# Seven products of halves for z1 in a Fourier-mixing and gated-MLP layer, with h2 stored turned

## The chip, the cores and the metric

The kernel runs on one core of one Trainium2 chip. The time is the device time of one execution in microseconds (us), as the median of several runs. The engines are TensorE (PE in the profile; its weight loads PEld), VectorE (DVE), ScalarE (ACT), GpSimd (POOL) and SyncE (SP), which only issues transfers.

## The reference

Sequence 2048, width 512, fp32. The two parts and what lies around them, cut:

```python
mod = (silu(c) @ w_mod).reshape(1, 6, 1, -1)          # sa, ca, ga, sb, cb, gb
h = layernorm(x) * (1 + ca) + sa
y = dft_seq_re @ (h @ dft_hid_re.T) - dft_seq_im @ (h @ dft_hid_im.T)
x = x + ga * y
h = layernorm(x) * (1 + cb) + sb                       # "h2" in the kernel
z = gelu(h @ w_in)                                     # 512 -> 1792
z1, z2 = z[..., :896], layernorm(z[..., 896:])
g = w_sp @ z2 + b_sp[:, None]                          # w_sp is 2048 x 2048
x = x + gb * ((z1 * g) @ w_out)                        # 896 -> 512
```

## The kernel before

Each fp32 product is made of three matmuls on a high and a low part (`matmul3`: high x high, high x low, low x high). The high part is an ACT copy to the PE's rounded type (`ah` of a streamed block, `prep_hi`), the low part a DVE subtraction (`al`, `prep_lo`); both stand in small rings of buffers. The names carry the block's number: al131 is the low part of block 131.

The streamed blocks are numbered n, and TensorE works through them in order. Blocks 0 to 127 (N2 = 128) are the DFT stage: `mm_a(n)` multiplies h by a block of the sequence DFT matrices, four quarters t of 512 tokens. For each tile (t, i) of 128 tokens, `mm_y` multiplies by the width DFT; then `post_y` adds x and takes statistics (DVE, with the factors on POOL), `norm_y` applies them (ACT), and `post_h` multiplies and adds the modulation (DVE, then POOL) and stores the tile of h2. The tiles of the quarters t = 0 to 2 are done between later blocks; those of t = 3 come after block 127, at N2 - 0.25, one after the other.

Then z1 (N2 to N3): h2's quarters are loaded back and turned by DVE as 128 x 512 blocks (`turn_block`), since the contraction must lie on partitions; 4 quarters x 7 column chunks x 4 k x 3 matmuls. Then z2 (N3 to N4), in seven products of halves (`mm_z2`), and w_sp times z2, also in seven products (`mm_w`); the sums of w_sp's quarters that this needs are made ahead in 16 units (`load_s`, `sum_s`), stored to `s_d` and streamed back. Last comes the product with w_out (`mm_o`).

The order is written out by hand: `at(n, f, ...)` puts a step behind block n, and `run(n)` emits what is due. Each engine runs its instructions in this order, so a step that waits holds back what is behind it on its engine. The buffers of the stages follow each other in the same memory: `change_s` closes the row buffers of the DFT stage and opens the slots of the later stages.

Of the passage into z1 these lines set the place of al131 (N2 + 3), for i = 2 and 3 of the last quarter:

```python
if i == 2:
    at(N2 - 0.25, prep, N2)
if i == 3:
    at(N2 - 0.25, prep_lo, N2 + 3)
at(N2 - 0.25, post_y, t, i)
at(N2 - 0.25, norm_y, t, i)
at(N2 - 0.25, post_h, t, i)
```

Of the kernel before, what the change touches and what calls it, by code (L numbers as in the profile page):

```python
# [19 lines left out]
def fnet_gmlp_kernel(  # L20
# [62 lines left out]
    h2_d = [dram.tile([Q, D], F32, name=f"h2_d{t}") for t in range(NQ)]  # L83
# [56 lines left out]
    src += h2_d + h2_d[:1]  # L140
    N3 = N2 + 4 * NQ
# [5 lines left out]
    NB = {p: N4 + 4 * NQ * i for i, p in enumerate(PROD)}  # L147
    stage, T, AH, AL = {}, {}, {}, {}
# [37 lines left out]
    def turn_block(dst, b, k):  # L186

        nc.vector.transpose(dst.rearrange("p (k a i) -> p a k i", k=4, i=32),
                            stage[b][:, :, 32 * k:32 * k + 32].rearrange("p (a k) i -> p a k i", k=4))
        if k == 3:  # L190
            stage.pop(b)
            load(b + 2)

# [3 lines left out]
    slots, TT, S2 = [], {}, {}  # L197

    def again(k):
        TT[k, 0] = slot(12 + k, f"tt0_{k}")  # L200
        turn_block(TT[k, 0], len(src) - 1, k)

    def form3(gg, kk):
        t = TT[kk, gg]
        nc.vector.tensor_tensor(t, TT[kk, 2 + gg], t, op=ALU.subtract)

    def prep_hi(n):
        if n >= NE:
            return
        if N3 <= n < N4:  # L210
            p = ZPROD[(n - N3) // 4]
            gg, kk = divmod((n - N3) % 4, 2)
            if p == 6:
                T[n] = S2[gg, kk] = bpool[0].tile([P, Q], F32, tag=("bh", "bl")[kk], bufs=3, name=f"s2_{gg}{kk}")
                nc.vector.tensor_tensor(T[n], TT[2 + kk, gg], TT[kk, gg], op=ALU.subtract)
            else:
                T[n] = TT[kk + (2 if p in (2, 4, 3) else 0), gg + (2 if p in (1, 2, 5) else 0)]
        else:
            b, k = divmod(n, 4) if n < N3 else (len(src) + (n - N4) // 4, (n - N4) % 4)
            if N2 + 4 <= n < N3:  # L220
                g = (n - N2) // 4
                T[n] = TT[k, g] = slot(4 * g + k - 4, f"tt{g}_{k}")
            else:
                T[n] = blocks.tile([P, Q], F32, tag="t", bufs=2, name=f"t{n}")
            if n >= N4:
                squares(T[n], stage[b][:, k % 2], k // 2)
            elif n < N2:
                squares(T[n], stage[b], k)
            else:
                turn_block(T[n], b, k)  # L230
        AH[n] = blocks.tile([P, Q], F32R, tag="ah", bufs=4, name=f"ah{n}")
        nc.scalar.activation(AH[n], T[n], AF.Copy)  # L232
        if not N2 <= n < N4 and k == 3:
            stage.pop(b)
            load(b + 2)
# [3 lines left out]
    def prep_lo(n):  # L239
# [3 lines left out]
        if N3 <= n < N4 and (n - N3) % 4 == 3:  # L243
            AL[n] = slot(16, f"al{n}", F32R)
# [295 lines left out]
    def post_h(t, i):  # L540
# [3 lines left out]
        nc.gpsimd.dma_start(h2_d[t][i * P:(i + 1) * P, :], h2)  # L544


    wi_hi, wi_lo, wraw, ZT = {}, {}, {}, {}
    z_hi, z_lo, Z, ZN = {}, {}, {}, {}

    WJ, W2 = {}, []  # L550

    def load_wi(e, k0):

        if e == 0:
            raw = wpool[0].tile([P, 2, FH], F32, tag="wj", bufs=2, name=f"wraw{k0}")
        else:
            if not W2:
                W2.append(wpool[0].tile([P, ND, FH], F32, name="w2"))
            raw = W2[0][:, k0:k0 + 2, :]
        v = w_in.rearrange("(a k i) f -> a i k f", a=4, i=32)  # L560
        for a in range(4):
            nc.sync.dma_start(raw[32 * a:32 * a + 32], v[a][:, k0:k0 + 2, e * FH:(e + 1) * FH])
        if e == 0:
            for k in range(2):
                wraw[k0 + k] = raw[:, k, :]

    def make_wi(k):
        wi_hi[k] = wpool[1].tile([P, FH], F32R, name=f"wih{k}")
        wi_lo[k] = wpool[1].tile([P, FH], F32R, name=f"wil{k}")
        nc.scalar.activation(wi_hi[k], wraw[k], AF.Copy)  # L570

    def make_wi_lo(k):
        nc.vector.tensor_tensor(wi_lo[k], wraw.pop(k), wi_hi[k].bitcast(F32), op=ALU.subtract)
# [3 lines left out]
    def parts_w2():  # L577
        w = W2[0]
        return w[:, :2, E0], w[:, :2, E1], w[:, 2:, E0], w[:, 2:, E1]

    def form_w23():
        b11, b12, b21, b22 = parts_w2()
        nc.vector.tensor_tensor(b12, b22, b12, op=ALU.subtract)
        nc.vector.tensor_tensor(b11, b11, b12, op=ALU.add)

    def form_w14():
        t2, _, b21, b22 = parts_w2()
        W2.append(wpool[0].tile([P, 2, ZP], F32, name="w2s"))
        nc.vector.tensor_tensor(W2[1], b22, t2, op=ALU.subtract)
        nc.vector.tensor_tensor(t2, b21, t2, op=ALU.subtract)  # L590

    def form_w(p):
        return W2[1] if p == 5 else parts_w2()[{1: 0, 6: 0, 7: 1, 2: 2, 4: 0, 3: 3}[p]]

    def hi_w(p):
        WJ[p] = wpool[0].tile([P, 2, 2, Q], F32R, tag="wj", bufs=2, name=f"wj{p}")
        nc.scalar.activation(WJ[p][:, 0, :, :ZP], form_w(p), AF.Copy)

    def lo_w(p):
        hi, lo = WJ[p][:, 0, :, :ZP], WJ[p][:, 1, :, :ZP]  # L600
        nc.vector.tensor_tensor(lo, form_w(p), hi.bitcast(F32), op=ALU.subtract)

    def mm_z1(ns):
        g, k0 = divmod(ns[0] - N2, ND)
        if k0 == 0:
            for f in range(NF):
                ZT[f] = bank((NF * g + f) % 8, f"z1p{g}_{f}")
        a = [(k0 + m, AH.pop(n), AL.pop(n)) for m, n in enumerate(ns)]
        for f in range(NF):
            cols = slice(f * P, (f + 1) * P)  # L610
            for k, th, tl in a:
                matmul3(ZT[f], wi_hi[k][:, cols], wi_lo[k][:, cols], th, tl, k == 0, k == ND - 1)
        if k == ND - 1:
            for f in range(NF):
                z = zrow[0].tile([P, Q], F32, tag="z1row", bufs=NF, name=f"z1_{g}_{f}")
                nc.scalar.activation(z.rearrange("p (a k i) -> p k a i", a=4, i=32),
                                     ZT.pop(f).rearrange("p (k a i) -> p k a i", k=4, i=32), AF.Gelu_apprx_tanh)
# [52 lines left out]
    def sum_s(r, g, b, first):  # L670
        a11, a12, a21, a22 = [SJ[r, g, b][:, i] for i in range(4)]
# [39 lines left out]
    def mm_w(n):  # L711
# [206 lines left out]
    for j, load_at, n, m, k, plus_one in ((2, 41, 49, 50, 7, False), (4, 52, 56, 58, 7, True),  # L918
                                          (3, 60, 65, 66, 7, False), (5, 68, 85, 86, 6, False)):
# [5 lines left out]
    for t in range(NQ):  # L925
        n = 8 * NQ * (t + 1)
        for i in range(4):
# [7 lines left out]
            if t < NQ - 1:  # L935
                at(y + 1, post_y, t, i)
                at(y + 2, norm_y, t, i)
                at(y + 3 if t else 71 + i, post_h, t, i)
                if i < 2:
                    at(y + 2 if t else y + 3, load_xr, t, i + 2)  # L940
            else:
                if i == 2:
                    at(N2 - 0.25, prep, N2)
                if i == 3:
                    at(N2 - 0.25, prep_lo, N2 + 3)
                at(N2 - 0.25, post_y, t, i)
# [30 lines left out]
    at(90, change_q)  # L977
    at(N2, change_s)
    when = [(90 + 4 * i, 3) for i in range(9)] + [(N2 + d, 6) for d in (4, 7, 10, 13, 17, 21, 25)]
# [10 lines left out]

    at(N2 + 1, load_wi, 1, 0)
    at(N2 + 2, load_wi, 1, 2)
    at(N2 + 6, hi_w, 1)
    at(N2 + 7, lo_w, 1)
    at(N2 + 9, form_w23)
    at(N2 + 10, hi_w, 6)
    at(N2 + 10, lo_w, 6)
    at(N2 + 12, form_w14)
    for k, d in ((0, 10), (2, 11), (1, 12), (3, 13)):
        at(N2 + d, again, k)  # L1000
    for gg in range(2):
        for kk in range(2):
            at(N2 + 14 + gg, form3, gg, kk)
            at(N3 + 4 + 2 * gg + kk, form1, gg, kk)
    for n in range(N2, N3):
        prep(n)
        run(n)
        two_first(mm_z1, n, n - N2, ND)
# [76 lines left out]
    for o in range(len(order)):  # L1085
# [53 lines left out]
```

## Time and profile before

| | us |
|---|---|
| median of 3 runs | 949.32 (948.85 to 950.26) |
| the profiled execution | 948.71 |
| its span | 946.8 |
| PE busy in the span | 938.3 (99%) |
| DVE / ACT / POOL busy | 712.3 / 391.7 / 168.2 |
| z1, from its first to its last matmul | 448.2 to 524.4 |
| z2 | 524.4 to 593.7 |

The span is the part of the execution that the profile's instructions cover; 1.9 us lie around it. The granted clock of TensorE is 1.0 throughout. In the rows of the profile a line such as L248 is the line of the kernel, "al<-t,ah" is what is written and read, x244 the number of instructions; in a time line the bracket gives the idle time before an instruction and what ended it.

### The profile page before, as it was taken

The page shows a single profiled execution, that of the slowest core. Times are in us where ns is not written, and L with a number is a line of the kernel's source. Part 1 is how long each engine was busy: PE and PEld are TensorE (multiplying, and loading weights), DVE is VectorE, ACT ScalarE, POOL GpSimd, SP SyncE. Part 2 cuts the span into 40 slices and gives each one's busy share as a digit, 9 for nine tenths or more (in the row PEclk, how much of TensorE's full clock was granted, in tenths as well). Part 3 has the DMA queues.
Part 4 walks back from the last instruction along what each step waited for, and adds up shares of the span by engine and source line. Part 5 has one row for each costly group of instructions (what it writes and reads, how often), then busy time and mean ns, then how long its engine had stood idle before and what let it go on. Part 6 is the DMA issues. An engine that isn't in the chain of part 4 may idle for free.

```text
span 946.8 us, 12325 instructions
## 1 busy us (share of the span) xinstructions
PE 938.3 (99%) x4150; PEld 778.9 (82%) x4150; DVE 712.3 (75%) x1156; ACT 391.7 (41%) x680; POOL 168.2 (18%) x330
## 2 busy tenths in 40 slices
PE   8999999999999999999999999999999999999998
PEld 5888888888888888888888998888888888888886
DVE  6789957775566767876537778999799889886662
ACT  4685424242132222322433768765545444331221
POOL 2330000111520154223412421332000000000000
PEclk9999999999999999999999999999999999999999
DMA  9996662667435877993887920544555465744541
GB/s 203 223 224 127 136 145 67 167 164 180 134 100 144 246 225 212 283 324 144 230 315 225 373 117 20 133 91 102 143 125 121 101 155 118 195 103 153 180 176 55
DMA packets 243343, 158.11 MB, mean 167 GB/s; under 512 B 130000, under 2 KB 212176, under 8 KB 243152
## 3 DMA queue, kind: packets, MB, share of 16 engines
q1 hardware_dynamic: 231520, 119.70, 51.7%
q0 software_dynamic: 11424, 37.24, 10.6%
q8 instruction: 32, 0.52, 0.2%
q10 hardware_dynamic: 336, 0.39, 0.1%
q14 instruction: 31, 0.25, 0.1%
HBM read 120.59 MB, written 36.70 MB: 166 GB/s over the span
## 4 chain that ended last, share of the span: by engine, by line
PE 97%; DVE 1%; ACT 1%; DMA 1%; POOL 0%; issue 0%; SPq 0%; DVEq 0%
PE gp L96 12%; PE gp L97 12%; PE gp L95 12%; PE gw L97 10%; PE gw L96 10%; PE gw L95 10%; PE yp L95 3%; PE yp L97 3%; PE yp L96 3%; PE op L96 3%; PE op L95 3%; PE z1p L97 3%; PE z1p L95 3%; PE op L97 3%; PE z1p L96 3%; PE z2p L97 2%
## 5 line engine op out<-in xcount | busy, mean ns | idle before, releaser
L232 ACT ACTIVATE ah<-t 128x512 fp32r<-128x512 f32 x244 | 154.0, 632 | 373.6 <-DVE t L175 234.7
L248 DVE TENSOR_TENSOR al<-t,ah 128x512 fp32r<-128x512 f32 x244 | 164.8, 676 | 70.9 <-PE gp L96 45.5
L95 PE MATMUL gp<-ah,hh 128*128 128x512 f32 x496 | 192.9, 389 | 0.0
L96 PE MATMUL gp<-al,hh 128*128 128x512 f32 x496 | 192.9, 389 | 0.0
L97 PE MATMUL gp<-ah,hl 128*128 128x512 f32 x496 | 192.9, 389 | 0.0
L175 DVE STREAM_TRANSPOSE t<-stage 128x512 f32<-128x512 f32 x240 | 168.9, 704 | 9.5 <-DMA stage<-in_A_dft_seq_re_dram 4.1
L97 PE MATMUL gw<-ah,bl 128*128 128x512 f32 x400 | 155.8, 390 | 0.3 <-DVE bl L709 0.3
L96 PE MATMUL gw<-al,bh 128*128 128x512 f32 x400 | 155.7, 389 | 0.0
L95 PE MATMUL gw<-ah,bh 128*128 128x512 f32 x400 | 155.6, 389 | 0.0
L95 PEld LDWEIGHTS gp<-ah,hh 128*128 128x128 f32 x496 | 93.1, 188 | 19.4
L97 PEld LDWEIGHTS gp<-ah,hl 128*128 128x128 f32 x496 | 93.1, 188 | 19.3
L96 PEld LDWEIGHTS gp<-al,hh 128*128 128x128 f32 x496 | 93.1, 188 | 19.3
L97 PEld LDWEIGHTS gw<-ah,bl 128*128 128x128 f32 x400 | 75.1, 188 | 16.4 <-DVE bl L709 1.0
L96 PEld LDWEIGHTS gw<-al,bh 128*128 128x128 f32 x400 | 75.1, 188 | 15.7
L95 PEld LDWEIGHTS gw<-ah,bh 128*128 128x128 f32 x400 | 75.1, 188 | 15.6
L681 POOL DMA_DIRECT2D s_d<-sj x64 | 34.8, 544 | 130.1 <-DVE sj L673 97.2
L248 DVE TENSOR_TENSOR al<-tt,ah 128x512 fp32r<-128x512 f32 x36 | 23.9, 683 | 38.6 <-PE z1p L96 28.6
L95 PE MATMUL yp<-hth,gh 128*128 128x512 f32 x128 | 49.8, 389 | 0.0
L96 PE MATMUL yp<-htl,gh 128*128 128x512 f32 x128 | 49.8, 389 | 0.0
L97 PE MATMUL yp<-hth,gl 128*128 128x512 f32 x128 | 49.8, 389 | 0.0
L95 PE MATMUL z1p<-ah,wih 128*128 128x512 f32 x112 | 43.6, 389 | 0.0
L96 PE MATMUL z1p<-al,wih 128*128 128x512 f32 x112 | 43.6, 389 | 0.0
(171 smaller groups left out, 1400.8 us busy)
## 6 DMA issues: line engine op xcount, KB each, us to landing
stage<-in_A_dft_seq_im_dram SPq DMA_DIRECT2D x64, 256.0 KB, 5.3
sj<-in_B_w_sp_dram SPq DMA_DIRECT2D x32, 512.0 KB, 7.3
s_d<-sj POOLq DMA_DIRECT2D x64, 256.0 KB, 4.9
stage<-s_d SPq DMA_DIRECT2D x128, 128.0 KB, 2.7
stage<-in_A_dft_seq_re_dram SPq DMA_DIRECT2D x60, 256.0 KB, 5.0
stage<-in_B_w_sp_dram SPq DMA_DIRECT2D x96, 128.0 KB, 3.3
z_d<-z POOLq DMA_DIRECT2D x28, 256.0 KB, 5.7
stage<-h_d SPq DMA_DIRECT2D x20, 256.0 KB, 6.7
```

Source lines behind the costliest of these rows:

```text
L95: nc.tensor.matmul(acc, ah, bh, start=first, stop=False, skip_group_check=go_on)
L96: nc.tensor.matmul(acc, ah, bl, start=False, stop=False, skip_group_check=go_on)
L97: nc.tensor.matmul(acc, al, bh, start=False, stop=last, skip_group_check=go_on)
L175: nc.vector.transpose(dst.rearrange("p (b i) -> p b i", i=32), block[:, :, 32 * k:32 * k + 32])
L232: nc.scalar.activation(AH[n], T[n], AF.Copy)
L248: nc.vector.tensor_tensor(AL[n], t, AH[n].bitcast(F32), op=ALU.subtract)
L681: nc.gpsimd.dma_start(s_d[m, r, g][b * P:(b + 1) * P, :], a)
```

## The change

- The first six of z1's seven column chunks are made by seven products of halves (`YPROD`), with three chunks, two halves of the tokens (gg) and two k blocks each. The sums of h2's quarters that they need (`form_t`, `make_x`) are those that z2 uses too, and stay in the slots; the sums of the weights are made by `form_v`. The seventh chunk stays a plain product (`mm_f7`), fitted between them. z1 now has 28 blocks and 300 matmuls, where it had 16 blocks and 336.
- PSUM results of the products 1, 6 and 7 are copied out by ACT; product 2 is followed by six copies back into PSUM, which product 4 goes on from; products 5 and 3 are added by DVE.
- h2 is stored turned: `turn_h` transposes a finished tile on DVE into `hturn` (one buffer) and stores it by four POOL transfers of 64 KB, in pieces of 128 bytes, to `ht_d` [width, tokens]. Before, `post_h` stored it by one POOL transfer. z1's blocks are then loaded as they are, and the twenty DVE transposes of `turn_block` go.
- The low parts of blocks N2 + 3, N2 + 7 and so on to N4 use slot 0, which exists only after `change_s`; `change_s` is called once the DFT stage is written out.
- w_in's halves are loaded as natural rows, two transfers for each half.
- Eleven of the 16 w_sp units are in the DFT stage (from n = 82, every 4 blocks; nine from n = 90 before), and the last modulation row is summed at 74 and 76.
- The columns of w_sp's quarters, the order of PSUM banks and two loads of w_sp are changed to fit.

On DVE, at the passage from the DFT stage into z1 (h2_3_i is tile i of the last quarter, y its y, xr its x, mod4 the modulation, wil the low part of a weight), before:

```order
L542 TENSOR_TENSOR h2_3_2_4145<-h2_3_2_4145,mod4_2060 128x512
L573 TENSOR_TENSOR wil2_4151<-wraw2_4068,wih2_4150 128x896
L573 TENSOR_TENSOR wil3_4155<-wraw2_4068,wih3_4154 128x896
L248 TENSOR_TENSOR al131_4158<-t131_4121,ah131_4128 128x512
L531 TENSOR_TENSOR y3_3_4160<-yp3_3_0_4027,mod2_1784 128x512
L532 TENSOR_TENSOR xr3_3_4115<-y3_3_4160,xr3_3_4115 128x512
L103 BN_STATS bsty_4164<-xr3_3_4115 128x6
L105 BN_AGGR mvy_4166<-bsty_4164 128x2
L542 TENSOR_TENSOR h2_3_3_4173<-h2_3_3_4173,mod4_2060 128x512
```

and after (vj is a part of a product's weights, w7 the seventh chunk's):

```order
L557 TENSOR_TENSOR h2_3_2_4205<-h2_3_2_4205,mod4_2060 128x512
L606 TENSOR_TENSOR vj2_4215<-w1_4135,vj2_4215 128x2x384
L614 TENSOR_TENSOR w7_4185<-w1_4135,w7_4185 128x256
L546 TENSOR_TENSOR y3_3_4220<-yp3_3_0_4099,mod2_1784 128x512
L547 TENSOR_TENSOR xr3_3_4183<-y3_3_4220,xr3_3_4183 128x512
L103 BN_STATS bsty_4224<-xr3_3_4183 128x6
L105 BN_AGGR mvy_4226<-bsty_4224 128x2
L564 STREAM_TRANSPOSE hturn3_2_4235<-h2_3_2_4205 128x512
L557 TENSOR_TENSOR h2_3_3_4233<-h2_3_3_4233,mod4_2060 128x512
L564 STREAM_TRANSPOSE hturn3_3_4243<-h2_3_3_4233 128x512
L265 TENSOR_TENSOR al131_4261<-xb0_3845,ah131_4188 128x512
```

al131 stood ahead of the last tile's five instructions; now it stands behind them and behind the turns of the last two tiles.

On POOL, the same place (nmry is the last factor of a tile's statistics), before:

```order
L115 TENSOR_SCALAR nmry_4143<-mvy_4138,rsy_4140 128x1
L543 TENSOR_TENSOR h2_3_2_4145<-h2_3_2_4145,mod3_2270 128x512
L544 DMA h2_d3_83<-h2_3_2_4145 128x512
L533 DMA x2_d3_79<-xr3_3_4115 128x512
L107 TENSOR_SCALAR mvy_4166<-mvy_4166 128x1
L108 TENSOR_TENSOR rsy_4168<-mvy_4166,mhalf_122 128x1
L115 TENSOR_SCALAR nmry_4171<-mvy_4166,rsy_4168 128x1
L543 TENSOR_TENSOR h2_3_3_4173<-h2_3_3_4173,mod3_2270 128x512
L544 DMA h2_d3_83<-h2_3_3_4173 128x512
```

and after:

```order
L567 DMA ht_d3_83<-hturn3_1_4207 32x16x32 x4
L558 TENSOR_TENSOR h2_3_2_4205<-h2_3_2_4205,mod3_2270 128x512
L548 DMA x2_d3_79<-xr3_3_4183 128x512
L107 TENSOR_SCALAR mvy_4226<-mvy_4226 128x1
L108 TENSOR_TENSOR rsy_4228<-mvy_4226,mhalf_122 128x1
L115 TENSOR_SCALAR nmry_4231<-mvy_4226,rsy_4228 128x1
L567 DMA ht_d3_83<-hturn3_2_4235 32x16x32 x4
L558 TENSOR_TENSOR h2_3_3_4233<-h2_3_3_4233,mod3_2270 128x512
L567 DMA ht_d3_83<-hturn3_3_4243 32x16x32 x4
```

Each tile's store is four transfers for one, and the store of a tile stands ahead of the next tile's addition.

On TensorE, after, where the second half of the first product begins (f7p0 is the seventh chunk of the first quarter):

```order
L97 MATMUL f7p0_4292<-ah129_3972,w7_4185 128x512
L95 MATMUL z1p1_10_4319<-ah130_3992,vj1_4157 128x512
L96 MATMUL z1p1_10_4319<-al130_4190,vj1_4157 128x512
L97 MATMUL z1p1_10_4319<-ah130_3992,vj1_4157 128x512
L95 MATMUL z1p1_10_4319<-ah131_4188,vj1_4157 128x512
L96 MATMUL z1p1_10_4319<-al131_4261,vj1_4157 128x512
```

Ahead of the first row stand z1's first 23 matmuls, on the blocks 128 and 129; al131 is read by the 29th. Before, the blocks 128 and 129 had all seven chunks, 42 matmuls.

The diff, cut:

```diff
-        nc.gpsimd.dma_start(h2_d[t][i * P:(i + 1) * P, :], h2)
+    def turn_h(t, i):
+        h2 = LN.pop((t, i))
+        ht = GP_[0].tile([P, D], F32, tag="hturn", bufs=1, name=f"hturn{t}_{i}")
+        nc.vector.transpose(ht.rearrange("p (b i) -> p b i", i=32), h2.rearrange("p (b i) -> p b i", i=32))
+        v = ht_d[t].rearrange("(b c) (a i r) -> a i c b r", c=32, a=4, i=4)
+        for a in range(4):
+            nc.gpsimd.dma_start(v[a, i], ht[32 * a:32 * a + 32].rearrange("c (b r) -> c b r", r=32))
...
+    YPROD = (1, 2, 6, 7, 4, 5, 3)
+    N3 = N2 + 4 * len(YPROD)
...
+    def form_t(n):
+        stage1 = n < N3
+        p = (YPROD if stage1 else ZPROD)[(n - (N2 if stage1 else N3)) // 4]
+        gg, kk = divmod(n % 4, 2)
+        a, b, c, d = TT[kk, gg], TT[2 + kk, gg], TT.get((kk, 2 + gg)), TT.get((2 + kk, 2 + gg))
...
-        if N3 <= n < N4 and (n - N3) % 4 == 3:
-            AL[n] = slot(16, f"al{n}", F32R)
+        if N2 <= n < N4 and n % 4 == 3:
+            AL[n] = slot(0, f"al{n}", F32R)
...
+    def mm_z1(n):
+        p = YPROD[(n - N2) // 4]
+        gg = n % 4 // 2
+        fresh = p in (1, 5)
+        a = [(AH.pop(m), AL.pop(m)) for m in (n, n + 1)]
+        if p in (2, 3):
+            for kk, t in enumerate(a):
+                mm_f7(gg if p == 2 else 2 + gg, 2 + kk, *t)
+        for f in range(3):
...
+                matmul3(ZT[gg, f], WJ[1, p][:, 0, kk, cols], WJ[1, p][:, 1, kk, cols], th, tl,
+                        fresh and kk == 0, kk == 1, not fresh)
+        if p == 1:
+            for kk, t in enumerate(a):
+                mm_f7(gg, kk, *t)
+        for f in range(3):
+            empty_z1(p, gg, f)
...
+                at(y + 4 if t else 72 + 2 * i, turn_h, t, i)
...
                 if i == 2:
                     at(N2 - 0.25, prep, N2)
-                if i == 3:
-                    at(N2 - 0.25, prep_lo, N2 + 3)
                 at(N2 - 0.25, post_y, t, i)
                 at(N2 - 0.25, norm_y, t, i)
+                if i:
+                    at(N2 - 0.25, turn_h, t, i - 1)
                 at(N2 - 0.25, post_h, t, i)
...
+                for f, *a in (((hi_v, 1), (lo_v, 1)), ((make_w7, 0),), ((hi_v, 2), (lo_v, 2), (make_w7, 1)), ((turn_h, t, 3),))[i]:
+                    at(N2 - 0.25, f, *a)
...
-    at(90, change_q)
-    at(N2, change_s)
-    when = [(90 + 4 * i, 3) for i in range(9)] + [(N2 + d, 6) for d in (4, 7, 10, 13, 17, 21, 25)]
+    at(80, change_q)
+    when = [(82 + 4 * i, 3) for i in range(11)] + [(N2 + 6, 8), (N2 + 14, 8), (N2 + 22, 8), (N3 + 4, 6), (N3 + 10, 6)]
...
+    change_s()
...
     for n in range(N2, N3):
         prep(n)
+        if n % 2 == 0:
+            prep_lo(n + 3)
         run(n)
-        two_first(mm_z1, n, n - N2, ND)
+        if n % 2 == 0:
+            mm_z1(n)
```

283 lines of the change are left out of this document (169 added, 114 removed).

## The prediction

> **What bounds the kernel now.** I read the page's busy times and its chain first, then TensorE's waits, then the stages by window.
>
> ```profile
> PE 938.3 (99%) x4150; PEld 778.9 (82%) x4150; DVE 712.3 (75%) x1156; ACT 391.7 (41%) x680; POOL 168.2 (18%) x330
> PE 97%; DVE 1%; ACT 1%; DMA 1%; POOL 0%; issue 0%; SPq 0%; DVEq 0%
> PE gp L432 <- ACT ah L232: 1.8, 1, 1.8
> PE busyp L337 <- DVE busy L276: 1.5, 1, 1.5
> PE z2p L95 <- ACT ah L232: 0.6, 1, 0.6
> PE gw L97 <- DVE bl L709: 0.3, 1, 0.3
> PE gp L432 <- ACT hh L408: 0.3, 1, 0.3
> 448.20:524.40 76.20, 76.20 (x338) 63.06 (x337) 42.29 (x62) 30.28 (x50) 24.81 (x46) 1.00 0.84 260
> 524.40:593.70 69.30, 68.68 (x338) 62.92 (x337) 57.08 (x92) 52.36 (x99) 15.74 (x32) 1.00 0.41 155
> L95 PE MATMUL z1p<-ah,wih x112: 389/389/389, 448.2 to 523.7; 128*128 128x512 f32 x112
> ```
>
> TensorE is busy 99% of the span, is 97% of the chain, and waits 4.5 us in all (1.8, 1.5, 0.6, 0.3, 0.3). So the time is the number of matmuls times their pace, plus any new wait. The two windows are the stages z1 and z2 (span, then busy time of PE, PEld, DVE, ACT, POOL, clock, DMA share, GB/s). z1 is 3 x 112 = 336 matmuls in 76.2 us without a gap: 0.2268 us each. DVE has 34 us to spare there, ACT 46, POOL 51.
>
> **The saving.** z1 becomes seven products of 2 halves of tokens x 3 column chunks x 2 k x 3 passes = 252 matmuls, plus 48 for the seventh chunk: 300 for 336. 36 x 0.2268 = **-8.2 us**. Nothing else leaves TensorE, so this bounds the gain; the twenty block transposes that go stood on DVE, beside matmuls.
>
> **The new wait, at the passage from the DFT stage into z1.** Before, DVE makes al131 ahead of the last tile of h2, as these rows of its and POOL's time line show.
>
> ```profile
> 436.66 0.69 DVE L542 TENSOR_TENSOR h<-h,mod 128x512 f32<-128x512 f32 x1 [2.18 <-ACT h L119]
> 437.50 2.17 DVE L573 TENSOR_TENSOR wil<-wraw,wih 128x896 fp32r<-128x896 f32 x1
> 444.17 0.69 DVE L542 TENSOR_TENSOR h<-h,mod 128x512 f32<-128x512 f32 x1 [2.17 <-ACT h L119]
> 447.11 0.70 DVE L188 STREAM_TRANSPOSE t<-stage 128x512 f32<-128x512 f32 x1
> 453.73 3.17 DVE L573 TENSOR_TENSOR wil<-wraw,wih 128x896 fp32r<-128x896 f32 x2 [0.15 <-ACT wih L570]
> 457.05 0.69 DVE L248 TENSOR_TENSOR al<-t,ah 128x512 fp32r<-128x512 f32 x1
> 457.66 0.68 DVE L531 TENSOR_TENSOR y<-yp,mod 128x512 f32<-128x512 f32 x1
> 459.89 0.18 DVE L105 BATCH_NORM_AGGREGATE mvy<-bsty 128x2 f32<-128x6 f32 x1
> 462.25 0.69 DVE L542 TENSOR_TENSOR h<-h,mod 128x512 f32<-128x512 f32 x1 [2.17 <-ACT h L119]
> 437.43 1.29 POOL L543 TENSOR_TENSOR h<-h,mod 128x512 f32<-128x512 f32 x1 [1.66 <-DVE h L542]
> 461.10 0.26 POOL L115 TENSOR_SCALAR nmry<-mvy,rsy 128x1 f32<-128x1 f32 x1
> 463.02 1.30 POOL L543 TENSOR_TENSOR h<-h,mod 128x512 f32<-128x512 f32 x1 [1.66 <-DVE h L542]
> 464.62 0.63 POOL L544 DMA_DIRECT2D h_d<-h  x1 [0.30 <-POOL h L543]
> ```
>
> After the change al131 shares a buffer that opens only when the DFT stage's row buffers close, so on DVE it stands behind the last tile's statistics, its h2 multiply and the turns of tiles (3,2) and (3,3). TensorE wants it early: from 448.2 (the end of the y products, which don't change) it has 18 + 6 matmuls of the first half and 4 more, 28 x 0.2268 = 6.35 us, so from **454.55**.
>
> When is it ready? By the last tile's rows (y 457.66, aggregate to 460.07, nmry to 461.36, multiply from 462.25), from the start of y: statistics done after 2.4, POOL's factors after 3.7, h2 multiply from 4.6 to 5.3 us.
> - Multiply (3,1) stays at 444.17 to 444.86. Two short pieces follow (w7's low part, a 256-column subtraction, about 0.35; al130, 0.69): y(3,2) starts at 445.9, its multiply ends at 445.9 + 5.3 = 451.2. Behind that are vj2's low part (768 columns; 1.86 at the pace of the 2.17 us row, which ran beside POOL's add, 0.9 at that of the pair in 3.17) and the rest of w7 (0.35 to 0.7). y(3,3) starts at 454.2 (452.5 at the quick pace).
> - Statistics done 456.6. Turn (3,2), 0.70: 456.6 to 457.3. h2 multiply (3,3): 458.8 to 459.5.
> - POOL: factors at 457.9, then four issues of turn (3,2)'s store, then the add of (3,3). The DMA rows:
>
> ```profile
> L544 POOL DMA_DIRECT2D h_d<-h x16 | 9.5, 592 | 4.7 <-POOL h L543 4.7
> L458 POOL DMA_DIRECT2D hrow_d<-w0r x2 | 1.2, 609 | 40.7 <-ACT w0r L463 40.7
> stage<-s_d SPq DMA_DIRECT2D x128, 128.0 KB, 2.7
> h_d<-h POOLq DMA_DIRECT2D x16, 256.0 KB, 3.1
> x_d<-xr POOLq DMA_DIRECT2D x16, 256.0 KB, 2.3
> z_d<-z POOLq DMA_DIRECT2D x28, 256.0 KB, 5.7
> ```
>
> An issue on POOL takes 0.6 us whether it is one row of 2 KB (609 ns) or 128 rows (592): I take 0.6 for the new ones, of 512 pieces of 128 bytes. Four: 457.9 to 460.3; the add, 1.30: to 461.6. Landing after an issue: 2.7, from s_d's loads, which are 512 pieces too (of 256 bytes); ends 2.3 and 5.7. The last issue starts at 459.7 and lands at 462.4. There is one hturn buffer, so turn (3,3) waits for that landing: 462.4 to 463.1.
> - al131, 0.69 and gaps: **464.0**. TensorE waits 464.0 - 454.55 = **9.5 us**. With the quick pace, issues of 0.55 and a landing of 2.3 al131 comes at 460.7 to 461.6, a wait of 6.1 to 7.1; with landing 5.7 it is 12.5.
>
> A rule speaks for the long end: the Trainium skill, "DMA: Bandwidth & Descriptors" (Specifications), asks for pieces of at least 512 bytes for line rate, with a read-modify-write below. By it these 64 KB move like four times as much, as an estimate from that page, and h_d's 256 KB row (3.1) would stand for 2.7: 0.4 us more. No run here yet shows 128-byte stores.
>
> **The restart.** TensorE's first matmuls of the program, and its first after a short wait:
>
> ```profile
> L337 PE MATMUL busyp<-busy,ones x10: 592/592/1193, 1.5 to 7.2; 128*128 128x512 f32 x10
> 1.53:5.00 3.47, 3.47 (x4) 1.48 (x5) 0.23 (x1) 1.49 (x2) 0.00 (x0) 1.00 0.67 190
> 9.59 1.19 PE L432 MATMUL gp<-ah,hh 128*128 128x512 f32 x4 [1.81 <-ACT ah L232]
> ```
>
> The same matmul took 1193 ns at first and 592 later, half speed for about 3.47 us, while the granted clock reads 1.00; after 1.81 us of waiting four others took 1.19 with no such slowness. A 9.5 us wait is far longer than 1.81, so I take the program's start: half speed over 3.47 us loses **1.7 us** (bounds 0 and 1.7).
>
> **The rest of z1.** Per pair of k blocks TensorE needs 18 x 0.2268 = 4.1 us; ACT must give two ah, three copies out of PSUM and half a weight part, DVE two al and half a part.
>
> ```profile
> L232 ACT ACTIVATE ah<-t 128x512 fp32r<-128x512 f32 x244 | 154.0, 632 | 373.6 <-DVE t L175 234.7
> L616 ACT ACTIVATE z<-z1p x28: 582/598/660, 467.7 to 524.6; 128x512 f32<-128x512 f32 x28
> L248 DVE TENSOR_TENSOR al<-t,ah 128x512 fp32r<-128x512 f32 x244 | 164.8, 676 | 70.9 <-PE gp L96 45.5
> ```
>
> A part has 768 columns, 0.95 at ah's pace on ACT and 0.9 to 1.86 on DVE, half of it per pair. ACT: 2 x 0.63 + 3 x 0.60 + 0.5 = 3.6; DVE: 2 x 0.68 + 0.9 = 2.3, and in the last two products three additions out of PSUM more, some 2 us. It fits, though closely at the end. z2's start waited 0.6 before; I take **1.0 us** of small waits at such joints (0.3 to 3).
>
> **The DFT stage, n = 72 to 81.** Eight turns go through the one buffer, in a stretch in which TensorE did not wait and POOL was busy 23.8 of 56 us:
>
> ```profile
> 228.00:284.00 56.00, 56.00 (x249) 46.37 (x248) 33.74 (x54) 13.25 (x21) 23.82 (x35) 1.00 0.45 127
> DVE al L248 <- PE gp L96: 45.5, 37, 4.1
> ```
>
> A turn's cycle is 0.7 + 0.1 + 3 x 0.6 + 2.7 = 5.3 us, seven of them 37 us in a stretch of 40; DVE's lead on TensorE there, 4.1 us in its longest wait, covers unevenness. I take **0.3 us** (0 to 3). The w_sp units, two more in this stage, hide in the same lead; that the other loads come straight from turned rows costs nothing, since nothing asks for them before al131.
>
> **Sum**: -8.2 + 9.5 + 1.7 + 1.0 + 0.3 = +4.3 on the profiled execution's 948.7: 953.0. The median of the runs is 0.6 above that execution, so **953.6**.
>
> **Rivals.**
> 1. *Faster.* The chain to al131 runs at its least: the quick pace, landing 2.3, a wait of 6.1, no restart, and the two old waits (0.6 and 0.3) go: -8.2 + 6.1 - 0.9 = -3.0, **946.3**. It decides if al131 is done before about 460.8. For it: the pair in 3.17 us shows the quick pace. Against: four issues, an add, a landing and a turn in series. The Trainium skill, "TensorE: Matmul & The Clock Gate" (Part 1: The HAM clock gate), goes against it: half clock after about 3.4 us idle and for as long after; by that rule 6.1 us of waiting also costs the 1.7, and 948.0 is left. Chance 0.13.
> 2. *The two cancel.* A wait of 7 to 8.5, small waits 0.3 to 1, no or half a restart: -1 to +1.3, about **949.5**. For it: the quick pace at any one of the steps. Chance 0.17.
> 3. *POOL's issue grows with its pieces.* No row has 512 pieces on POOL. At 1.2 us an issue, the four of each tile push the adds and the tiles behind: al131 at about 467, a wait of 12.5, and turns in the DFT stage of 7.1 us, 7 x 7.1 - 40 - 4.1 = 5.6 over: -8.2 + 12.5 + 1.7 + 1.0 + 4 to 5.6 = +11 to +12.6, about **960.5**. Against: 609 ns for one piece, 592 for 128. Chance 0.10.
>
> The forecast (wait 8.5 to 11, restart) has 0.60. About 0.2%, 1.9 us, is what a measurement of this kernel can tell from no change: faster 0.13, same 0.17, slower 0.70. The range runs from rival 1 to rival 3: 946.5 to 960.5; the slower cases alone lie between 951.5 and 960.5.
>
> **What would show it.** Right: TensorE's waits show one at z1p for DVE's al, of 6 to 12 us near 454.5; DVE waits before the last turn on ht_d's landing; the first matmuls after it show half speed; z1 otherwise keeps 0.227 us a matmul. Wrong: no such wait (then 941 to 943); POOL issues of ht_d of 1 us and more; gaps in TensorE around n = 72 to 81; many waits of ah, al or PSUM copies through z1 or z2.

## The result: 963.54 us, 1.45% slower

| | before | changed |
|---|---|---|
| median, us | 949.12 (948.85 to 950.26, 4 runs) | 963.54 (961.22 to 964.28, 4 runs) |
| ratio | | 1.0145 (95%: 1.0126 to 1.0165) |
| the profiled execution; its span | 948.71; 946.8 | 961.22; 959.4 |
| z1's first matmul | 448.2 | 454.4 |
| z2's first matmul | 524.4 | 535.4 |
| first matmul of the w_sp product | 593.7 | 606.6 |

The way was forecast, the size was not: 953.6 with a range to 960.5. The profiled execution of the changed kernel is the fastest of its four. Its span is 12.6 us longer: 6.2 before z1 begins, 4.8 in z1 (81.0 for 76.2), 1.9 in z2 (71.2 for 69.3), and 0.3 less behind.

The busy times on the page after:

```profile
PE 936.5 (98%) x4114; PEld 774.2 (81%) x4114; DVE 738.0 (77%) x1197; ACT 413.6 (43%) x725; POOL 204.4 (21%) x378
```

TensorE's longer waits in the view of waits, and one of DVE's (in total, times, longest):

```profile
PE z1p L96 <- DVE al L265: 9.7, 1, 9.7
PE gp L95 <- DVE gl L91: 2.4, 1, 2.4
PE gp L96 <- DVE al L265: 1.7, 1, 1.7
PE z2p L95 <- ACT ah L249: 1.4, 1, 1.4
DVE hturn L564 <- DMA ht_d<-hturn: 20.6, 5, 6.2
```

The first wait is the one forecast at the passage into z1. The next two are new, in the DFT stage, and the last row points to a cause: DVE waited 20.6 us for the stores of turned tiles to land, 15.9 of them in the DFT stage. DVE's, POOL's and TensorE's rows in the time line at both places (start and length in us; the wait before it in brackets):

```profile
250.46 0.70 DVE L564 STREAM_TRANSPOSE hturn<-h 128x512 f32<-128x512 f32 x1
260.13 0.71 DVE L564 STREAM_TRANSPOSE hturn<-h 128x512 f32<-128x512 f32 x1 [6.21 <-DMA ht_d<-hturn]
271.68 0.71 DVE L564 STREAM_TRANSPOSE hturn<-h 128x512 f32<-128x512 f32 x1 [3.51 <-DMA ht_d<-hturn]
289.33 0.71 DVE L564 STREAM_TRANSPOSE hturn<-h 128x512 f32<-128x512 f32 x1 [6.18 <-DMA ht_d<-hturn]
460.48 0.68 DVE L546 TENSOR_TENSOR y<-yp,mod 128x512 f32<-128x512 f32 x1
463.95 0.71 DVE L564 STREAM_TRANSPOSE hturn<-h 128x512 f32<-128x512 f32 x1 [1.12 <-DMA ht_d<-hturn]
469.26 0.71 DVE L564 STREAM_TRANSPOSE hturn<-h 128x512 f32<-128x512 f32 x1 [3.55 <-DMA ht_d<-hturn]
251.82 2.68 POOL L567 DMA_DIRECT2D ht_d<-hturn  x4 [0.21 <-DVE t L186]
470.59 0.80 PE L96 MATMUL z1p<-al,vj 128*128 128x512 f32 x1 [9.67 <-DVE al L265]
```

The issues of these stores, of which the time line shows four in one row, in the view of the tile ht_d (ns of one: least, median, most):

```profile
L567 POOL DMA_DIRECT2D ht_d<-hturn x64: 648/651/751, 231.6 to 473.4; - x64
```

A turn's cycle through the one buffer was 9.7 us from 250.46 to 260.13, not 5.3. The four issues took 2.68 us (0.65 each, where 0.6 was assumed); the last of them was out at 254.5 and DVE stood until 260.1.

Stretches of the same trace (span, then busy PE, PEld, DVE, ACT, POOL, granted clock, share of the DMA engines, GB/s): three in which DVE waited for a landing, then the two half-speed stretches.

```profile
254.50:260.10 5.60, 5.60 (x26) 4.66 (x25) 0.00 (x0) 0.00 (x0) 0.58 (x1) 1.00 0.80 210
268.00:271.70 3.70, 3.70 (x18) 3.04 (x18) 0.19 (x2) 0.56 (x2) 2.07 (x4) 1.00 0.34 71
284.00:289.30 5.30, 5.30 (x25) 4.21 (x23) 0.00 (x0) 0.00 (x0) 1.17 (x1) 1.00 1.09 327
279.50:282.70 3.20, 3.20 (x9) 2.42 (x9) 3.20 (x7) 0.84 (x3) 1.53 (x3) 0.50 0.27 80
470.60:474.00 3.40, 3.40 (x8) 2.75 (x9) 2.97 (x4) 0.60 (x1) 2.51 (x4) 0.51 0.19 39
```

Where a landing took 6 us the DMA engines were 0.80 and 1.09 busy, with block loads of the DFT matrices under way in both stretches and two 512 KB loads of w_sp in the last; where they were 0.34 busy it took 2.1. That these loads held the stores is read from these rows; of the loads of w_sp alone, e4 below is a trial. In the middle stretch DVE waited 3.5 us although the store landed quickly. At clock 0.50 TensorE made 9 matmuls in 3.20 us.

### The profile page after: what moved, and what is told of

Its sections match the earlier page's. It is cut to its first block, busy times and chain, and to the rows that moved or that the text cites. A ratio compares the mean times of both kernels' runs of the same rounds, so it can differ in the third digit from the quotient of the medians.

```text
span 959.4 us, 12378 instructions
## 1 busy us (share of the span) xinstructions
PE 936.5 (98%) x4114; PEld 774.2 (81%) x4114; DVE 738.0 (77%) x1197; ACT 413.6 (43%) x725; POOL 204.4 (21%) x378
## 4 chain that ended last, share of the span: by engine, by line
PE 48%; DVE 2%; ACT 1%; POOL 1%; DMA 1%; issue 1%; DVEq 0%; POOLq 0%; ACTq 0%
PE gw L97 10%; PE gw L95 9%; PE gw L96 9%; PE op L95 3%; PE op L96 3%; PE op L97 3%; PE z1p L96 2%; PE z1p L97 2%; PE z1p L95 2%; PE z2p L97 2%; PE z2p L96 2%; PE z2p L95 2%; DMA ht_d<-hturn 1%; DVE al L265 1%; DVE z L742 0%
## 5 line engine op out<-in xcount | busy, mean ns | idle before, releaser
L249 ACT ACTIVATE ah<-t 128x512 fp32r<-128x512 f32 x248 | 156.4, 631 | 373.3 <-DVE t L186 259.6
L265 DVE TENSOR_TENSOR al<-t,ah 128x512 fp32r<-128x512 f32 x248 | 167.4, 676 | 64.0 <-PE gp L96 38.0
L567 POOL DMA_DIRECT2D ht_d<-hturn x64 | 42.2, 665 | 31.1 <-DVE hturn L564 25.9
L95 PE MATMUL op<-woh,uh 128*128 128x512 f32 x112 | 43.6, 389 | 0.0
L96 PE MATMUL op<-wol,uh 128*128 128x512 f32 x112 | 43.6, 389 | 0.0
```

The costliest lines, as they stand in the source:

```text
L95: nc.tensor.matmul(acc, ah, bh, start=first, stop=False, skip_group_check=go_on)
L96: nc.tensor.matmul(acc, ah, bl, start=False, stop=False, skip_group_check=go_on)
L265: nc.vector.tensor_tensor(AL[n], t, AH[n].bitcast(F32), op=ALU.subtract)
L567: nc.gpsimd.dma_start(v[a, i], ht[32 * a:32 * a + 32].rearrange("c (b r) -> c b r", r=32))
```

## The experiments

The theory: both losses come from places on DVE. One hturn buffer puts landings on DVE's path in the DFT stage, and al131's place puts the last tile's chain on TensorE's path. The rivals: the extra POOL issues and w_sp units slow the stage whatever the buffer; the waits only move on. z1's length is taken from its first matmul to z2's first. Each edit is shown against the kernel it starts from: e1, e2 and e4 start from the changed kernel, e5 from e3, e6 from e5, e7 and e8 from e6, e9 and e10 from e8, e11 from e10, e12 from e11.

| run | median, us | ratio to before (95%) | z1 starts | z1 length |
|---|---|---|---|---|
| before | 949.0 | | 448.2 | 76.2 |
| changed | 963.54 | 1.0145 (1.0126 to 1.0165) | 454.4 | 81.0 |
| e1_two_buffers | 956.16 | 1.0075 (1.0060 to 1.0090) | 448.3 | 80.5 |
| e2_lows_first | 958.31 | 1.0098 (1.0083 to 1.0113) | 453.6 | 77.6 |
| e3_both | 950.75 | 1.0019 (1.0009 to 1.0029) | 448.4 | 77.7 |
| e4_units_back | 964.71 | 1.0169 (1.0152 to 1.0186) | 454.0 | 81.6 |
| e5_sums_early | 954.66 | 1.0063 (1.0048 to 1.0078) | 448.6 | 81.9 |
| e6_table_early | 955.64 | 1.0069 (1.0052 to 1.0086) | 448.1 | 81.5 |
| e7_z2_operands | 957.65 | 1.0090 (1.0075 to 1.0105) | 448.5 | 80.8 |
| e8_low_in_place | 951.63 | 1.0027 (1.0018 to 1.0036) | 448.2 | 77.2 |
| e9_one_buffer_dft | 959.41 | 1.0112 (1.0098 to 1.0126) | 453.9 | 78.3 |
| e10_quarter3_later | 959.17 | 1.0109 (1.0092 to 1.0126) | 448.0 | 83.5 |
| e11_lows_prompt | 948.28 | 0.9994 (0.9985 to 1.0003) | 449.7 | 74.3 |
| e12_copies_later | 947.49 | 0.9988 (0.9979 to 0.9997) | 448.6 | 73.1 |

**e1_two_buffers**: half of the turns in place.

```diff
-        ht = GP_[0].tile([P, D], F32, tag="hturn", bufs=1, name=f"hturn{t}_{i}")
+        inplace = (t, i) in ((0, 1), (0, 2), (0, 3), (1, 3), (2, 1), (2, 3), (3, 1), (3, 3))
+        ht = h2 if inplace else GP_[0].tile([P, D], F32, tag="hturn", bufs=1, name=f"hturn{t}_{i}")
```

> The turn no longer has one buffer: tiles (0,1), (0,2), (0,3), (1,3) and the odd tiles of the quarters 2 and 3 are transposed in place, the others through hturn, so that a turn never waits for the store of the turn just ahead of it. Theory (one buffer makes DVE wait for a landing): DVE's waits for ht_d's landing (20.6 us) fall under 3, TensorE's two waits near 278 and 291 go with their half-speed stretch, z1 starts at 448.2 +-1 (454.4 in the changed kernel). At the passage into z1 little is won, since POOL's addition of tile (3,3) ends 0.3 us before the landing: the wait for al131 stays at 8 to 9.5 us. Time about 956 (954.5 to 958). Rival (four POOL issues for one, and two more w_sp units in the DFT stage, slow DVE whatever the buffer): z1 still starts after 452, time 961 to 964.

TensorE's waits of this run; the two in the DFT stage and the half-speed stretch are gone, and no wait of DVE for ht_d is left:

```profile
PE z1p L96 <- DVE al L265: 8.7, 1, 8.7
PE busyp L352 <- DVE busy L291: 1.5, 1, 1.5
PE z2p L95 <- ACT ah L249: 1.4, 1, 1.4
PE gp L447 <- ACT ah L249: 1.2, 1, 1.2
```

956.16, as the theory had it, with the wait at the passage 1.0 us shorter. The POOL issues are the same in number, and the w_sp units stand where they stood, so neither slows the DFT stage without the one buffer.

**e4_units_back**: nine w_sp units from n = 90.

```diff
-    when = [(82 + 4 * i, 3) for i in range(11)] + [(N2 + 6, 8), (N2 + 14, 8), (N2 + 22, 8), (N3 + 4, 6), (N3 + 10, 6)]
+    when = [(90 + 4 * i, 3) for i in range(9)] + [(N2 + 6, 8), (N2 + 10, 8), (N2 + 14, 8), (N2 + 18, 8), (N2 + 22, 8), (N3 + 4, 6), (N3 + 10, 6)]
```

> The changed kernel with nine w_sp units in the DFT stage from n = 90 on, as before the change, and two more in z1. Theory (single buffer): z1 starts within 1.5 us of 454.4, time 961 to 965. Rival (the units moved ahead bring their loads and stores into the stretch of the turns and delay the landings): the waits near 278 and 291 shrink to under half, z1 starts at 449 to 451.5, time 957 to 961.

TensorE's two waits in the DFT stage, and DVE's wait at the last turn there:

```profile
PE gp L95 <- DVE gl L91: 2.5, 1, 2.5
PE gp L96 <- DVE al L265: 0.4, 1, 0.4
288.95 0.71 DVE L564 STREAM_TRANSPOSE hturn<-h 128x512 f32<-128x512 f32 x1 [4.80 <-DMA ht_d<-hturn]
```

z1 starts at 454.0 and the time is 964.71, so the units are not the main cause. They have a part in it: without their loads there DVE's last wait fell from 6.2 to 4.8 and TensorE's second from 1.7 to 0.4, while the first stayed. z1's start shows only 0.4 us of that, since the profiled execution began its first product 0.8 us later (10.20 for 9.38).

**e2_lows_first**: al131 to al134 ahead of the last turns.

```diff
-        if N2 <= n < N4 and n % 4 == 3:
+        if N2 + 4 <= n < N4 and n % 4 == 3:
...
+                if i == 3:
+                    at(N2 - 0.25, prep, N2 + 1)
                 at(N2 - 0.25, post_y, t, i)
+                if i == 3:
+                    at(N2 - 0.25, prep, N2 + 2)
                 at(N2 - 0.25, norm_y, t, i)
                 if i:
                     at(N2 - 0.25, turn_h, t, i - 1)
+                if i == 3:
+                    at(N2 - 0.25, prep, N2 + 3)
                 at(N2 - 0.25, post_h, t, i)
+                if i == 3:
+                    at(N2 - 0.25, prep, N2 + 4)
...
+    at(N2, prep_lo, N2 + 7)
```

> The low parts al131 to al134 stand on DVE ahead of the turns of the tiles (3,2) and (3,3) and use the ring of al; one hturn buffer as in the changed kernel. Theory (al131's place behind the turns is the wait of the passage): TensorE's wait of 9.7 us for al at z1p falls to 0 to 1.5, the half-speed stretch behind it goes, z1 takes 70 to 73 us from its first to its last matmul (81.0 in the changed kernel), the DFT stage keeps its loss (z1 starts near 454.4); time 952 to 954. Rival (whatever needs the last tile of h2 waits as long, so that the wait only moves to the blocks behind al131): z1 stays at 79 to 81 us, time 961 to 964.

**e3_both**: the edits of e1 and e2.

> Both edits: turns without the single buffer and al131 to al134 ahead of the last turns. Theory: the two losses are separate and add up; z1 starts at 448.2 +-1 and takes 70 to 73 us; with the small waits at the end of z1 and in z2 that the changed kernel has (3.4 us) the time is 945 to 947.5, below the kernel before. Rival (the two have one cause, so that one edit alone wins nearly all): as the better of the two alone, within 1.5 us.

TensorE's waits, of e2 in the first two rows, of e3 in the third:

```profile
PE z1p L96 <- DVE al L265: 0.3, 1, 0.3
PE f7p L95 <- ACT z1o L666: 5.6, 1, 5.6
```
```profile
PE f7p L95 <- ACT z1o L667: 3.4, 1, 3.4
```

The wait for al131 went from 9.7 to 0.3, but a new one of 5.6 us stands 44 matmuls further on, with its own half-speed stretch; it is for ACT's gelu of the first f7p (z1o). The rival is half right: e2 won 5.2 us where 9.5 to 11.5 were expected. The edits add up: 7.4 for e1, 5.2 for e2, 12.8 for both, of the 14.4 that the changed kernel lost. The saving did not show: e3's 950.75 missed its forecast of 945 to 947.5.

**e5_sums_early**: form_v(6) ahead of the last turn, hi_v and lo_v of product 6 one block later.

```diff
-                for f, *a in (((hi_v, 1), (lo_v, 1)), ((make_w7, 0),), ((hi_v, 2), (lo_v, 2), (make_w7, 1)), ((turn_h, t, 3),))[i]:
+                for f, *a in (((hi_v, 1), (lo_v, 1)), ((make_w7, 0),), ((hi_v, 2), (lo_v, 2), (make_w7, 1)), ((form_v, 6), (turn_h, t, 3)))[i]:
-    at(N2 + 2, form_v, 6)
-        at(N2 + 4 + 4 * i, hi_v, p)
-        at(N2 + 5 + 4 * i, lo_v, p)
+        at(N2 + 4 + 4 * i + (p == 6), hi_v, p)
+        at(N2 + 5 + 4 * i + (p == 6), lo_v, p)
```

> As the kernel with both edits, and the weights' sums for product 6 (form_v) stand on DVE ahead of the last turn, ACT's copy of them one block later. Theory (the new wait of 3.4 us at f7p is PSUM bank 6, held until ACT's gelu of the first f7p, which stands on ACT behind a copy that waits for DVE's sums, and so behind the last turn): ACT reaches the gelu after its copies and the table load, about 1.3 us earlier than before or more; the wait falls to 1 to 2.2 us; time 946 to 948.5. Rival (TensorE waits there for the turned quarter 2, xh, and not for the gelu): the wait stays above 3, time 950 to 952.

**e6_table_early**: a gelu of a small tile at N2 - 0.5.

```diff
+    at(N2 - 0.5, nc.scalar.activation, sc, sc, AF.Gelu_apprx_tanh)
```

> As e5_sums_early, and the gelu's table is loaded ahead, by a gelu of a 128x4 tile that nobody reads any more, before the last quarter's tiles. Theory: the table load of 1.28 us goes from between the copies and the first gelu; the wait at f7p falls by about as much, to 0 to 0.9; time 944 to 946.5. Rival: the wait is the same as in e5_sums_early, and so is the time within 0.7 us.

**e7_z2_operands**: two calls of `prep` ahead of `empty_z` for the second half of product 3.

```diff
+        if n == NZ[3] + 2:
+            prep(n + 1)
+            prep(n + 2)
```

> As e6_table_early, and the last two operands of z2's product 2 are formed and copied ahead of the additions and gelus of product 3. Theory (TensorE's 1.4 us wait in z2 is for ah behind eight ACT copies and gelus, since product 2's operand is now formed as late as that): the wait of 1.4 falls under 0.4, time 1.0 to 1.4 us below e6_table_early, 943 to 945.5. Rival (the additions, now behind, hold TensorE up in the same place or at the first blocks of the w_sp product): no gain, within 0.5 us of e6_table_early.

TensorE's waits, two rows of e5 and one each of e6 and e7:

```profile
PE z1p L97 <- DVE vj L607: 5.9, 1, 5.9
PE f7p L95 <- ACT z1o L667: 1.0, 1, 1.0
```
```profile
PE f7p L96 <- DVE xl L214: 1.2, 2, 0.8
```
```profile
PE z2p L97 <- DVE al L265: 2.0, 2, 1.6
```

The wait for the gelu fell to 1.0 in e5 and went in e6, as expected, but all three are slower than e3 and missed their times by 6 to 12 us. The edit of e5 had moved the low part of product 6's weights too, behind `make_x(1)` on DVE, which waits for the load of quarter 3; TensorE then waited 5.9 us for it. In e7 z2's wait only changed its place, from ah to al. Its expectation failed.

**e8_low_in_place**: the low part back behind its high part (`lo_v` of product 6 at N2 + 5).

```diff
-        at(N2 + 5 + 4 * i + (p == 6), lo_v, p)
+        at(N2 + 5 + 4 * i, lo_v, p)
```

> As e6_table_early, but the low part of product 6's weights stands on DVE ahead of the copies of the turned quarter 3 again, right behind its high part. Theory (the 5.9 us wait at z1p for vj came from where that low part had been put, behind operands that wait for quarter 3's load; with it out of the way the two losses of the change are gone and the saving of 8.2 us shows): no wait over 1.5 us between the DFT stage and the end of z1, z1 from its first to its last matmul 69 to 72 us, time 943.5 to 946.5, faster than the kernel before. Rival (the passage has a fixed debt of work, and each wait taken away returns behind it): another wait of 3 us or more in z1, time 948 to 953.

**e9_one_buffer_dft**: e8 with one buffer again for the quarters 0 to 2.

```diff
-        inplace = (t, i) in ((0, 1), (0, 2), (0, 3), (1, 3), (2, 1), (2, 3), (3, 1), (3, 3))
+        inplace = t == 3 and i % 2 == 1
```

> As e8_low_in_place, but in the quarters 0 to 2 all turns go through the one hturn buffer again, as in the changed kernel. Theory (the DFT stage's loss is the one buffer's and adds to the rest): DVE waits 10 to 18 us for ht_d's landings there, TensorE waits 3 to 5 us near 278 and 291, the time is 4 to 6.5 us above e8_low_in_place. Rival (the loss is made up later, since z1 then has its operands earlier): under 2 us above it.

The waits, of e8 in the first two rows, of e9 in the others:

```profile
PE z1p L95 <- ACT ah L249: 1.9, 1, 1.9
PE f7p L96 <- DVE xl L214: 1.2, 2, 0.9
```
```profile
PE gp L96 <- DVE al L265: 3.7, 1, 3.7
PE gp L95 <- DVE gl L91: 1.4, 1, 1.4
DVE hturn L565 <- DMA ht_d<-hturn: 15.3, 3, 6.5
```

e9 is 7.8 us above e8, more than the 6.5 expected, and z1 starts 5.7 later: the buffer's loss stands by itself. How close the turns come when no buffer holds them, four of e8's show:

```profile
250.62 0.70 DVE L565 STREAM_TRANSPOSE hturn<-h 128x512 f32<-128x512 f32 x1
254.00 0.70 DVE L565 STREAM_TRANSPOSE h<-h 128x512 f32<-128x512 f32 x1
263.27 0.70 DVE L565 STREAM_TRANSPOSE hturn<-h 128x512 f32<-128x512 f32 x1
265.06 0.70 DVE L565 STREAM_TRANSPOSE h<-h 128x512 f32<-128x512 f32 x1
```

The first two stand 3.4 us apart, the other two 1.8.

e8's 5.9 us wait went, but z1 still takes 77.2; two waits of 1.2 and 1.9 with a half-speed stretch are what ends there, both on the turned quarters. So the expectation of 943.5 to 946.5 failed, and the time, no better than e3's, is that of the rival, in which each wait taken away returns behind it, though its wait of 3 us or more did not come. I formed another theory: plain z1 read quarter 3 only with its last 84 matmuls, some 57 us after z1's start; the products read it after some 30, and the last tile's chain (statistics, turn, store, load, sums) takes that long.

**e10_quarter3_later**: another order of blocks, so that quarter 3 is read later. With it `make_x(1)` goes to where product 6's second half is formed, the high part of product 6's weights one block later and product 4's parts two; product 7's low part stays where it was.

```diff
+    def block(n):
+        p, gg = ((1, 0), (1, 1), (2, 0), (2, 1), (6, 0), (7, 0), (6, 1), (7, 1),
+                 (4, 0), (4, 1), (5, 0), (5, 1), (3, 0), (3, 1))[(n - N2) // 2]
+        return p, gg, n % 2
...
-            if n in (N2 + 4, N2 + 8):
+            if n in (N2 + 6, N2 + 10):
```

> As e8_low_in_place, with z1's blocks in another order: product 7 of the first half of the tokens ahead of product 6 of the second half, so that the turned quarter 3 is first read 12 to 24 matmuls (2.7 to 5.4 us) later, and the seventh chunk's parts of the quarters 2 and 3 (mm_x) one block later. Theory (what is left is one chain: the last tile of h2, its store, the load of quarter 3, its sums; the products read it some 30 us after z1's start where plain z1 read it after 57): the waits at xl (1.2 us) and at ah for product 6 (1.9 us) with its half-speed stretch go, z1 takes 70 to 73 us from its first to its last matmul (77.2 in e8_low_in_place), time 944 to 947.5, below the kernel before. Rival (ACT and DVE are the limit in this stretch, whatever the order): the waits move to the PSUM copies, z1 stays above 75.5 us, time 949 to 953.

**e11_lows_prompt**: the low parts of the weights of the products 7 and 4 behind their high parts (both at N2 + 7 and N2 + 13), form_v(5) and form_v(3) at N2 + 13 and N2 + 14.

```diff
-        at(N2 + 4 + 4 * i + {6: 1, 4: 2}.get(p, 0), hi_v, p)
-        at(N2 + 5 + 4 * i + {4: 2}.get(p, 0), lo_v, p)
+        at(N2 + {6: 5, 7: 7, 4: 13}.get(p, 4 + 4 * i), hi_v, p)
+        at(N2 + {6: 5, 7: 7, 4: 13}.get(p, 5 + 4 * i), lo_v, p)
```

> As e10_quarter3_later, with the low parts of product 7's and product 4's weights right behind their high parts (7 blocks and 13 blocks into z1) and the two later sums of weights behind them. Theory (what held e10_quarter3_later, two waits for vj of 5.9 and 1.7 us with a half-speed stretch, came from where its edits had put those low parts; the order of the blocks itself is right): both waits go, the one at the PSUM copies (1.1 us) may grow to 2; z1 takes 70.5 to 74 us from its first to its last matmul, time 945 to 948.5. Rival (ACT and DVE are the limit): the waits come back at other operands in the same stretch, z1 stays above 76 us, time 950 to 953.

**e12_copies_later**: ACT's three copies back into PSUM for the second half behind the copies of product 6's first half.

```diff
-        if p == 2:
+        back = {(2, 0): 0, (6, 0): 1}.get((p, gg))
+        if back is not None:
...
-                nc.scalar.activation(turned(ZT[gg, f]), natural(Z1.pop((1, gg, f))), AF.Copy)
+                nc.scalar.activation(turned(ZT[back, f]), natural(Z1.pop((1, back, f))), AF.Copy)
```

> As e11_lows_prompt, with ACT's three copies of the second half's sums back into PSUM behind the copies of product 6's first half, ahead of which they stood without being needed. Theory (the last wait in the passage, 1.15 us at the PSUM copies with a half-speed stretch behind it, is ACT's queue of 1.66 us ahead of those copies): the wait goes or falls under 0.5, the half-speed stretch near 482 with it, z1 takes 71 to 73.5 us from its first to its last matmul (74.3 in e11_lows_prompt), time 945 to 947.5, faster than the kernel before. Rival (the chain through quarter 3's sums is what ends there): waits of 1 us or more at al or ah of product 6's second half in its place, time within 1 us of e11_lows_prompt's 948.3.

TensorE's waits, one row of e10, two of e11, four of e12:

```profile
PE z1p L97 <- DVE vj L615: 7.5, 2, 5.9
```
```profile
PE gp L455 <- ACT ah L255: 2.4, 1, 2.4
PE z1p L95 <- ACT z L712: 1.1, 1, 1.1
```
```profile
PE gp L455 <- ACT ah L255: 2.3, 1, 2.3
PE z1p L96 <- DVE al L271: 1.5, 6, 0.3
PE z2p L95 <- ACT ah L255: 1.4, 1, 1.4
PE z1p L95 <- ACT ah L255: 0.6, 1, 0.6
```

e10 made the mistake of e5 again, with product 7's low part behind `make_x(1)` and so behind quarter 3's load (a wait of 5.9 us; the other, of 1.7, is for product 4's low part), and its forecast failed by 12. With that mended, e11 equals the kernel before (its runs spread from 947.46 to 950.25, and the profiled one has a wait of 2.4 at the program's start), and e12 is faster by a little: 947.49, ratio 0.9988 (0.9979 to 0.9997, just clear of 1), some 1.1 us. Its z1 takes 73.1 us, 3.1 less than before, with no wait above 0.64 and no half-speed stretch. The 300 matmuls by themselves are 68.0 at the pace of before; the other 5 us are some ten short stops of 0.1 to 0.8 for operands. z2 takes 71.1 us, 1.8 more than before, with the wait of 1.4 still in it. e11 changed the order of the blocks and the places of the low parts together, so what the order alone gives is not shown.

## Why the prediction was wrong

- **The saving** (-8.2): 36 matmuls fewer are there; no kernel tried showed more than 3.1 of it in z1's length.
- **The wait at the passage** (9.5): measured 9.7. The path was right: POOL's issues, its addition and DVE's wait before the last turn come in the order forecast, within 1.2 us of their times once these are shifted by the 6.2 us that z1 starts later. That the sum comes so near is partly luck. The steps listed for y of the last tile add up to 453.8 at most, not 454.2 (measured 460.48, less the shift 454.3). The low part of vj2 took 0.96 and not 1.86, that of w7 2.03 and not 0.35 to 0.7; turn (3,2) itself waited 1.1 us for a landing that the sum did not have; and its own store landed 2.1 us after its last issue, not 2.7.
- **The restart** (1.7): 8 matmuls at half speed in 3.4 us behind that wait, 1.6.
- **The DFT stage** (0.3, 3 at most): measured 6.2. This is the step that failed: the overlap of the turns' stores with DVE's other work. I had set seven cycles of 5.3 against a stretch of 40 us and let DVE's lead of 4.1 us cover the unevenness. Two things were wrong in it.
  - The distances: the turns do not come evenly. With free buffers all eight take 50 us, from 230.8 to 280.8, but two pairs stand 3.4 and 1.8 us apart (e8), so that even a cycle of 5.3 makes DVE wait some 1.9 and 3.5 us, as an estimate from these distances. The wait of 3.5 was measured, behind a store that landed in 2.1.
  - The landing: the 2.7 came from rows of another stage. In the other two of the three cycles landings reached 6.6 and 6.0, and DVE waited 6.2 both times, longer than its lead. In the kernel before, the eight stores of h_d in the same stretch (228 to 284) took 2.3 to 4.8 us to land, so a longer landing was there to be read.

  TensorE waited 2.4 and 1.7 for it, with a half-speed stretch between; I had priced half speed only behind the long wait. How the 6.2 divide between distances and landings is not shown. That the one buffer is the cause is: without it z1 starts at 448.3 and 448.2 (e1, e8), with it at 454.4 and 453.9 (the changed kernel, e9). Gaps of TensorE around n = 72 to 81 were among the prediction's own signs of being wrong.
- **Small waits** (1.0): about 1.6 in z1 (what its length leaves beside the other terms) and 1.9 more in z2. Mis-sized by some 2.5 us.
- **Rival 3** came nearest in its number (960.5), not in its mechanism: an issue took 0.65 us, and the path was lengthened by landings. Its own terms gave up to 961.9, where the range was ended at 960.5.
- **Rival 1** wanted a wait of 6.1 at the passage, rival 2 one of 7 to 8.5; with the order as it is, e1 shows 8.7 even with free buffers.

By the terms measured: 6.2 - 8.2 + 9.7 + 1.6 + 1.6 + 1.9 = 12.8, for 12.6 in the span. The medians differ by 14.4: the three runs without a profile are 2.1 to 3.1 us longer than the profiled one, and why is not shown.

## What to carry to other kernels

A product scheme that saves matmuls also asks for its last operand earlier: before counting matmuls, follow the chain from the last producer to its first reader under the new order, and place on the in-order engines every operand that TensorE needs soon ahead of whatever waits for a store or a load. A single staging buffer in front of a store puts that store's landing on the engine that fills it: price the landing from the slow transfers of the same stretch, and hold each cycle against the distance to the next use of the buffer, not the sum of the cycles against the stretch. A low part that came to stand behind a step that waits for a load cost 5.9 us twice here: in e5 it was moved behind that step, in e10 the step was moved ahead of it.

## What the runs showed of the hardware

- Half speed did not go by the length of the wait alone. Waits of 2.4 us (the changed kernel, in the DFT stage) and 1.4 (e1, in z2) were followed by half speed 1.5 and 1.6 us after the restart, the same wait of 1.4 in the changed kernel's z2 by none, one of 3.7 (e9, in the DFT stage) by none, and one of 3.4 (e3) by 5.7 us of it. The granted clock was 0.50 from 279.4 to 282.8 in the changed kernel and from 596.8 to 600.2 in e1, 3.4 us each, and from 468.13 to 474.96 in e3, 6.8 us, begun 1.2 us before TensorE's restart. Stretches (columns as above, the granted clock third from the right), of e1 behind its wait:

```profile
597.40:600.00 2.60, 2.60 (x9) 2.29 (x8) 2.15 (x5) 2.60 (x7) 1.00 (x3) 0.50 1.06 238
```

  Of e9 behind its wait of 3.7, at full clock:

```profile
290.80:296.00 5.20, 5.20 (x23) 4.29 (x24) 5.09 (x9) 1.97 (x4) 2.05 (x4) 1.00 0.63 147
```

  Of e3 behind its wait of 3.4:

```profile
469.30:475.00 5.70, 5.70 (x14) 4.46 (x15) 4.08 (x7) 4.92 (x10) 2.21 (x4) 0.50 0.74 218
```

  The Trainium skill, "TensorE: Matmul & The Clock Gate" (Part 1: The HAM clock gate), has a window of about 3.4 us that runs on its own and does not start with the work: the delayed starts and these lengths agree with that, while its condition of a whole idle window does not agree with the waits of 2.4 and 1.4 us.
- A DVE operation with two inputs beside POOL's addition took three times as long as its partner, and a store of POOL's was issued late while DVE ran such operations back to back; this is read from rows and was not tried. In e8 a sum of weights took 2.95 us beside the addition and its partner 0.96 after it, and the store of a turn that ended at 465.6 was issued at 467.1, DVE busy until then (its time line):

```profile
461.03 2.95 DVE L591 TENSOR_TENSOR w<-w 128x768 f32<-128x768 f32 x1
464.01 0.96 DVE L592 TENSOR_TENSOR w1e<-w 128x768 f32<-128x768 f32 x1
464.88 0.70 DVE L565 STREAM_TRANSPOSE h<-h 128x512 f32<-128x512 f32 x1
461.84 1.31 POOL L558 TENSOR_TENSOR h<-h,mod 128x512 f32<-128x512 f32 x1
467.11 2.58 POOL L568 DMA_DIRECT2D ht_d<-h  x4 [3.96 <-DVE xl L214]
```

- Stores of 64 KB in 512 pieces of 128 bytes were not slow by themselves: they took 2.1 us where the DMA engines were 0.34 busy (268.00 to 271.70 above), less than the 2.7 and 3.1 that the prediction weighed.
